# Weights, gated buffers and batch rows at other addresses in a fused FFT filter and gated feed-forward kernel

## The chip, the cores and the metric

The kernel runs on one core of a Trainium2 chip. The metric is the device time of one launch in microseconds. Before the change it is 1562.73 us, the median of three runs (1562.23 to 1562.77).

A core has five engines that the text names: TensorE (PE in the profile, its weight loads PEld), VectorE (DVE), ScalarE (ACT), GpSimd (POOL) and SyncE (SP, which issues most DMAs). SBUF is the on-chip memory of 128 partitions that all engines read. PSUM holds what PE accumulates.

## The reference

The input `x` has 8 batches of 3136 rows of 256 values. A filter is applied in the frequency domain along the rows, and the result goes through a gated feed-forward layer with a convolution of width 3 over the hidden rows:

```python
X = np.fft.rfft(x, axis=1)
y = np.fft.irfft(X * (filt_r + 1j * filt_i), n=3136, axis=1)
h = np.maximum(y @ w_in, 0.0)              # 256 -> 1024
conv = sum(conv_w[k] * hp[:, k:k + S, :] for k in range(3))
gate = 1.0 / (1.0 + np.exp(-conv))
out = (h * gate) @ w_out                   # 1024 -> 256
```

`hp` is `h` with a row of zeros at either end. `conv_w` has a weight per hidden feature and tap.

## The kernel before

**First stage** (until about 365 us). The transforms are matrix products with tables, in fp32. For each batch and pair of rows, PE runs L323, L334 (a transpose), L346 or L349, and L233. DVE multiplies with the filter (L358 to L360), POOL adds (L362), and the result goes through DRAM (`b_dram`) and comes back as `br`. The last table product (L215) gives `y`, transposed, in PSUM. ACT copies it to `y0` in fp32r, a 32-bit format in which PE needs one pass for a matmul, and DVE writes the remainder to `y1` (`last_out`, L146 and L149). In the same stage the weights are converted. `convert_weights` takes `w_in` and `w_out` in eight pieces; for each, ACT writes the leading part (`wi0`, `wo0`) and POOL the remainder (`wi1`, `wo1`, L152).

**Gated stage** (the rest). Rows are taken in chunks `j` of 896, two halves `i` of 448 in each, and for every chunk the 1024 hidden features in eight slices `f` of 128. One step `m` of the loop is one (j, f, i):

- `inner` (L454): six matmuls on 450 columns into a PSUM tile `ps_h`. For each of two halves `k` of the 256 features, `mm3` runs `wi0` with `y0` (L177), `wi0` with `y1` (L178), `wi1` with `y0` (L179). The `wi` slice is the weights that are loaded, and the `y` row is the operand that moves.
- `relu`, `conv`, `gate` (L465 to L478): ACT and DVE make the gated value `t`.
- `split_g` (L480): ACT writes its leading part to a buffer `g0`, POOL the remainder to `g1` (L152).
- `project` (L488): for each tile of 128 rows three matmuls on 256 columns into `po`: `g0` with `wo0` (L498), `g0` with `wo1` (L499), `g1` with `wo0` (L500). Here the `g` slice is loaded and the `wo` slice moves. Four tiles go with i = 0, three with i = 1.

The next batch's `y` is made between, in 14 pieces per batch (L215 and `last_out`). The order on the four compute engines is the order of this code, step by step (`manual_schedule`). `project` runs six steps behind `inner`.

**Where operands lie.** Pools place their tiles one after another in SBUF. An address here is a byte within a partition, the same on every partition. The table gives the remainder mod 256 of where each slice or row starts in the built program, before and after the change. Before, a slice of `wi` takes 512 bytes and one of `wo` 1024, so all slices have one remainder. A row `k` of a `y` tile takes 3138 x 4 = 12552 bytes, which is 8 above a multiple of 256. A half of 448 columns is 1792 bytes, a multiple of 256, and a `g` slice of 128 is 512 bytes, so neither changes a remainder.

| operand | before | after |
|---|---|---|
| `wi0`, `wi1`, slice f | 160 | 160 + 32 f |
| `wo0`, slice f | 160 | 160 + 32 f |
| `wo1`, slice f | 160 | 32 + 32 f |
| `y0`, rows k = 0, 1, even batch | 160, 168 | 192, 0 |
| `y1`, rows k = 0, 1, even batch | 192, 200 | 64, 128 |
| `y0`, rows k = 0, 1, odd batch | 160, 168 | 160, 224 |
| `y1`, rows k = 0, 1, odd batch | 192, 200 | 32, 96 |
| `g0`, by buffer | 224 (four) | 160, 0, 96, 192, 32 |
| `g1`, by buffer | 224 (four) | 128, 224, 64, 160, 0 |

Of the kernel before, what the change touches and what calls it, by code (L numbers as in the profile page):

```python
# [9 lines left out]
F32 = mybir.dt.float32  # L10
F32R = mybir.dt.float32r
# [5 lines left out]
S = 3136  # L17
# [3 lines left out]
D = 256  # L21
FF = 1024
KT = D // 128
NF = FF // 128
SUB = 448
# [99 lines left out]
def tile_fft_filter_gated_ffn(  # L125
# [16 lines left out]
    nc = tc.nc  # L142
    B = x.shape[0]

    def hi_act(dst, src):
        nc.scalar.activation(dst, src, AF.Copy)  # L146
# [4 lines left out]
    def lo_pool(dst, src, hi):  # L151
        nc.gpsimd.tensor_tensor(out=dst, in0=src, in1=hi.bitcast(F32), op=ALU.subtract)  # L152

    def to_f32(dst, raw, e, m):


        v = nc.vector
        pairs = raw.rearrange("p (n t) -> p n t", t=2)
        low, high = pairs[:, :, 0].bitcast(U32), pairs[:, :, 1]
        v.tensor_scalar(e, high, 3, 0x3FFFFFF8, op0=ALU.logical_shift_left, op1=ALU.bitwise_and)  # L160
        yield
        v.tensor_scalar(m, high, 30, 30, op0=ALU.logical_shift_right, op1=ALU.logical_shift_left)
        yield
        v.tensor_tensor(out=e, in0=e, in1=m, op=ALU.bitwise_or)
        yield
        v.tensor_scalar(m, high, 27, 0xF, op0=ALU.logical_shift_right, op1=ALU.bitwise_and)
        yield
        v.scalar_tensor_tensor(out=dst, in0=m, scalar=7.0, in1=e.bitcast(F32), op0=ALU.is_ge, op1=ALU.mult)
        yield
        v.tensor_scalar(e, dst.bitcast(I32), 23, 23, op0=ALU.logical_shift_right, op1=ALU.logical_shift_left)  # L170
        yield
        v.scalar_tensor_tensor(out=e.bitcast(F32), in0=low, scalar=2.0**-52, in1=e.bitcast(F32), op0=ALU.mult, op1=ALU.mult)
        yield
        nc.gpsimd.tensor_tensor(out=dst, in0=dst, in1=e.bitcast(F32), op=ALU.add)

    def mm3(ps, wh, wl, rh, rl, start=True, stop=True, **kw):
        nc.tensor.matmul(ps, lhsT=wh, rhs=rh, start=start, stop=False, **kw)  # L177
        nc.tensor.matmul(ps, lhsT=wh, rhs=rl, start=False, stop=False, **kw)  # L178
        nc.tensor.matmul(ps, lhsT=wl, rhs=rh, start=False, stop=stop, **kw)  # L179
# [4 lines left out]
    wc = ctx.enter_context(tc.tile_pool(name="wc", bufs=1))  # L184
# [1 line left out]
    cw = wc.tile([128, 3, NF], F32, name="cw")  # L186
    nc.gpsimd.memset(cw[:, 0, 0:1], 0.0)
    nc.scalar.activation(cw[:, 0, 0:1], cw[:, 0, 0:1], AF.Sigmoid)
    wi = [wc.tile([128, KT, FF], F32R, name=f"wi{h}") for h in range(2)]
    wo = [wc.tile([128, NF, D], F32R, name=f"wo{h}") for h in range(2)]  # L190


    ys, yps = {}, []
# [6 lines left out]

    def y_slices(b, sl):
        if sl.start == 0:
            ys[b] = [yps[b % 2].tile([128, KT, S + 2], F32R, name=f"y{h}") for h in range(2)]
            for t in ys[b]:
                nc.gpsimd.memset(t[:, :, 0:1].bitcast(F32), 0.0)
                nc.gpsimd.memset(t[:, :, S + 1:S + 2].bitcast(F32), 0.0)
        return (t[:, :, 1:S + 1].rearrange("p k (a c) -> p k c a", c=N2)[:, :, sl] for t in ys[b])
# [10 lines left out]
    def last_out(b, c):  # L218
        yh, yl = y_slices(b, slice(c, c + 2))
        pv = lasts.pop((b, c))[:, 0:4 * N1].rearrange("p (k c a) -> p k c a", c=2, a=N1)  # L220
        hi_act(yh, pv)
        lo_dve(yl, pv, yh)
# [5 lines left out]
    parts = {}  # L228
# [16 lines left out]
    with (  # L245
# [36 lines left out]
        def load_weights(k):  # L282
            raws[k] = raw = cv.tile([128, 2, 512], I32, name="raw")
            for part, src in enumerate((w_in, w_out)):
                nc.sync.dma_start(out=raw[:, part], in_=src[:, 512 * k:512 * k + 512])
# [6 lines left out]
        def convert_weights():  # L292

            for k in range(8):
                raw = raws.pop(k)
                em = cv.tile([128, 2, 512], I32, name="em", bufs=1)
                ws = cv.tile([128, 2, 256], F32, name="ws")
                yield from to_f32(ws.rearrange("p t n -> p (t n)"), raw.rearrange("p t n -> p (t n)"), em[:, 0], em[:, 1])
                yield
                parts = [[t.rearrange("p a b -> p (a b)")[:, 256 * k:256 * k + 256] for t in w] for w in (wi, wo)]  # L300
                for part, (wh, wl) in enumerate(parts):
                    hi_act(wh, ws[:, part])
                yield
                for part, (wh, wl) in enumerate(parts):
                    lo_pool(wl, ws[:, part], wh)
                yield
                if k < 6:
                    load_weights(k + 2)
# [68 lines left out]
        for i in range(XBUFS):  # L377
            load_first(i)
        csteps, wsteps = convert_conv(), convert_weights()
        done = NP * B + 1  # L380
        NI = done + N2 // 2 + 2
# [57 lines left out]
    wp = ctx.enter_context(tc.tile_pool(name="wp", bufs=2, reuse_waits="tile"))  # L439
# [4 lines left out]
    hs, ts, gs, pos = {}, {}, {}, {}  # L444
# [8 lines left out]

    def inner(j, f, i):  # L454
        ps = ps_h.tile([128, 512], F32, name="ps_h")[:, 0:SUB + 2]
        fs = slice(128 * f, 128 * f + 128)
        b, u = divmod(2 * j + i, NSUB)
        us = slice(u * SUB, u * SUB + SUB + 2)
        for k in range(KT):
            mm3(ps, wi[0][:, k, fs], wi[1][:, k, fs], ys[b][0][:, k, us], ys[b][1][:, k, us], start=k == 0, stop=k == KT - 1)  # L460
        hs[j, f, i] = ps

    def relu(j, f, i):
# [16 lines left out]
    def split_g(j, f, i):  # L480
        t = ts.pop((j, f, i))
        if i == 0:
            gs[j, f] = [wp.tile([128, 2 * SUB], F32R, name=f"g{h}", bufs=4) for h in range(2)]
        gh, gl = (g[:, i * SUB:i * SUB + SUB] for g in gs[j, f])
        hi_act(gh, t)
        lo_pool(gl, t, gh)

    def project(j, f, i):  # L488
        gh, gl = gs[j, f]
        if f == 0 and i == 0:  # L490
            pos[j] = [ps_o.tile([128, 512], F32, name=f"po{k}") for k in range(4)], wp.tile([128, NT, D], F32, name="ot")
        po, ot = pos[j]
        tiles = range(4) if i == 0 else range(4, NT)
        for t in tiles:
            o = po[t // 2][:, t % 2 * D:t % 2 * D + D]
            sl = slice(128 * t, 128 * t + 128)
            first, last = f == 0 and t % 2 == 0, f == NF - 1
            nc.tensor.matmul(o, lhsT=gh[:, sl], rhs=wo[0][:, f], start=first, stop=False, skip_group_check=True)  # L498
            nc.tensor.matmul(o, lhsT=gh[:, sl], rhs=wo[1][:, f], start=False, stop=False, skip_group_check=True)  # L499
            nc.tensor.matmul(o, lhsT=gl[:, sl], rhs=wo[0][:, f], start=False, stop=last, skip_group_check=True)  # L500

    def evacuate(j, f, i):
        if f < NF - 1:
# [17 lines left out]
    for b in range(1, B):  # L521
        start = ((NSUB * (b - 1) - 1) // 2 + 1) * 16 + (4 if b == 1 else 0)
        stop = NSUB * b // 2 * 16 + NSUB * b % 2
# [3 lines left out]
    with tc.manual_schedule(engines=COMPUTE):  # L527
        for m in range(NH + PLAG):
            if m + 4 in pieces:
                last_load(*pieces[m + 4])  # L530
            if a := at(m):
                inner(*a)
            if m in pieces:
                last_stage(*pieces[m], ps_h.tile([128, 512], F32, name="ps_h"))
            if 1 <= m < 4:
                pt = ps_o.tile([128, 512], F32, name=f"po{m}")[0:112].rearrange("p (n d) -> p n d", n=2)
                third(B - 1, NP - 4 + m, pt)
            if a := projected(m):
                project(*a)
            if a := at(m - 1):  # L540
                relu(*a)
                conv(*a)
            if a := at(m - 2):
                gate(*a)
            if a := at(m - 3):
                split_g(*a)
            if m in pieces:
                last_out(*pieces[m])
            if 1 <= m < 4:
                store(B - 1, NP - 4 + m, pt)  # L550
            if a := projected(m):
                evacuate(*a)
# [44 lines left out]
```

## Time and profile before

| | before |
|---|---|
| median of three runs | 1562.73 us |
| the profiled execution | 1559.94 us |
| its span | 1558.2 us |
| ACT busy, 0 to 330 us | 195.42 us |
| POOL busy, 0 to 330 us | 167.59 us |
| PE busy, 330 to 400 us | 64.70 us |

The profile is one execution. Its span runs from the first to the last instruction of the program, and the execution's own time stands beside it. In a row of the groups, "L177 PE MATMUL ps_h<-y,wi" names the line, the engine, the operation, what is written and what is read, then the shape, the number of instructions, their busy time in us, the mean length of one in ns, and the idle time of the engine before them with what ended it. Matmuls overlap: the record of one runs on beyond the start of the next. A row of the timeline gives start and length in us. A row of the chain of waits does the same for a piece of the work that ended last.

### The profile page before, as it was taken

How to read it: one execution, taken by the hardware profiler on the slowest of the kernel's cores; microseconds unless marked ns; L12 is line 12 of the kernel's file. 1: busy time of each engine (PE TensorE's matmuls, PEld its weight loads, DVE VectorE, ACT ScalarE, POOL GpSimd, SP SyncE). 2: the span in 40 equal slices, each digit the busy share in tenths (PEclk: the TensorE clock that was granted, in tenths of full speed). 3: DMA queues.
4: the chain of work that ended last, by engine and by line, in shares of the span. 5: the costliest groups of instructions: out<-in, count | busy, mean ns of one | idle time of the engine just before them, and what ended most of it. 6: DMA issues, size and time to landing. Idle time of an engine off the chain costs nothing.

```text
span 1558.2 us, 27801 instructions
## 1 busy us (share of the span) xinstructions
PE 1537.8 (99%) x10320; PEld 1418.2 (91%) x10320; DVE 1297.0 (83%) x1978; ACT 1245.0 (80%) x2274; POOL 703.0 (45%) x625
## 2 busy tenths in 40 slices
PE   8999999998999999999999999999999999999998
PEld 7787778877999999999999999999999999999998
DVE  3888888788888888888888888888888888888887
ACT  5655555566888888888888888888888888888887
POOL 3455555533444444444444444444444434444444
PEclk9999999999999999999999999999999999999999
DMA  9855555452111011111111011111011110100001
GB/s 236 261 179 168 172 169 164 137 148 78 33 52 48 31 47 48 49 49 47 48 42 36 27 53 52 44 48 48 31 48 42 49 54 27 46 25 25 24 25 48
DMA packets 89062, 115.24 MB, mean 74 GB/s; under 512 B 7400, under 2 KB 60168, under 8 KB 88928
## 3 DMA queue, kind: packets, MB, share of 16 engines
q1 hardware_dynamic: 74592, 87.77, 18.4%
q10 hardware_dynamic: 14336, 25.70, 5.8%
q8 instruction: 82, 1.34, 0.4%
q14 instruction: 52, 0.43, 0.1%
HBM read 62.06 MB, written 51.38 MB: 73 GB/s over the span
## 4 chain that ended last, share of the span: by engine, by line
PE 94%; DMA 2%; DVE 1%; ACT 1%; issue 0%; SPq 0%; POOL 0%; ACTq 0%; POOLq 0%; DVEq 0%
PE ps_h L178 12%; PE ps_h L179 12%; PE ps_h L177 11%; PE po L498 11%; PE po L500 11%; PE po L499 11%; PE ps L233 6%; PE ps_h L215 5%; PE pp L346 5%; PE ps L323 5%; PE ps L334 3%; DMA x<-in_x 1%; PE ps L215 1%; DVE y L149 1%; ACT y L146 0%; PE pp L349 0%
## 5 line engine op out<-in xcount | busy, mean ns | idle before, releaser
L152 POOL TENSOR_TENSOR g<-t,g 128x448 fp32r<-128x448 f32 x448 | 517.1, 1154 | 663.5 <-ACT g L146 259.3
L498 PE MATMUL po<-wo,g 128*128 128x256 f32 x1568 | 441.4, 282 | 0.0
L500 PE MATMUL po<-wo,g 128*128 128x256 f32 x1568 | 433.9, 277 | 0.4 <-POOL g L152 0.4
L499 PE MATMUL po<-wo,g 128*128 128x256 f32 x1568 | 433.4, 276 | 0.0
L472 DVE SCALAR_TENSOR_TENSOR t<-ps_h,cw,t 128x448 f32<-128x448 f32 x448 | 305.7, 682 | 85.6 <-ACT t L467 75.2
L178 PE MATMUL ps_h<-y,wi 128*128 128x450 f32 x896 | 330.3, 369 | 5.6 <-DVE y L149 5.6
L177 PE MATMUL ps_h<-y,wi 128*128 128x450 f32 x896 | 329.1, 367 | 3.3 <-DVE t L478 1.9
L179 PE MATMUL ps_h<-y,wi 128*128 128x450 f32 x896 | 328.8, 367 | 0.0
L473 DVE SCALAR_TENSOR_TENSOR t<-ps_h,cw,t 128x448 f32<-128x448 f32 x448 | 306.5, 684 | 16.0
L467 ACT ACTIVATE t<-ps_h,cw 128x448 f32<-128x448 f32 x448 | 284.8, 636 | 43.2 <-ACT ps_h L465 2.6
L498 PEld LDWEIGHTS po<-wo,g 128*128 128x128 f32 x1568 | 294.8, 188 | 7.1
L499 PEld LDWEIGHTS po<-wo,g 128*128 128x128 f32 x1568 | 294.3, 188 | 5.7
L500 PEld LDWEIGHTS po<-wo,g 128*128 128x128 f32 x1568 | 294.5, 188 | 0.6 <-POOL g L152 0.6
L465 ACT ACTIVATE ps_h<-ps_h 128x450 f32<-128x450 f32 x448 | 251.8, 562 | 32.9 <-PE ps_h L179 27.0
L478 DVE TENSOR_TENSOR t<-ps_h,t 128x448 f32<-128x448 f32 x448 | 275.3, 615 | 0.1
L477 ACT ACTIVATE t<-t 128x448 f32<-128x448 f32 x448 | 255.0, 569 | 12.4 <-DVE t L473 11.2
L146 ACT ACTIVATE g<-t 128x448 fp32r<-128x448 f32 x448 | 254.7, 568 | 0.2 <-DVE t L478 0.2
L362 POOL TENSOR_TENSOR z<-u,v 120x512 f32<-120x512 f32 x112 | 156.6, 1398 | 184.3 <-DVE v L360 154.1
L178 PEld LDWEIGHTS ps_h<-y,wi 128*128 128x128 f32 x896 | 168.3, 188 | 14.7 <-DVE y L149 7.9
L179 PEld LDWEIGHTS ps_h<-y,wi 128*128 128x128 f32 x896 | 168.3, 188 | 13.9
L177 PEld LDWEIGHTS ps_h<-y,wi 128*128 128x128 f32 x896 | 169.9, 190 | 11.7 <-DVE t L478 2.9
L149 DVE TENSOR_TENSOR y<-ps_h,y 128x448 fp32r<-128x448 f32 x98 | 103.1, 1053 | 75.3 <-ACT y L146 75.3
(62 smaller groups left out, 1661.6 us busy)
## 6 DMA issues: line engine op xcount, KB each, us to landing
x<-in_x SPq DMA_DIRECT2D x112, 224.0 KB, 2.9
b_dram<-sb ACTq DMA_DIRECT2D x112, 224.0 KB, 2.3
br<-b_dram SPq DMA_DIRECT2D x112, 224.0 KB, 2.6
out<-ot SPq DMA_DIRECT2D x27, 896.0 KB, 4.1
raw<-in_w_in SPq DMA_DIRECT2D x8, 256.0 KB
raw<-in_w_out SPq DMA_DIRECT2D x8, 256.0 KB
t_sb<-in_fr SPq DMA_DIRECT2D x15, 112.0 KB
t_sb<-in_fi SPq DMA_DIRECT2D x14, 112.0 KB
```

Of the source, the lines that this page charges most:

```text
L152: nc.gpsimd.tensor_tensor(out=dst, in0=src, in1=hi.bitcast(F32), op=ALU.subtract)
L177: nc.tensor.matmul(ps, lhsT=wh, rhs=rh, start=start, stop=False, **kw)
L178: nc.tensor.matmul(ps, lhsT=wh, rhs=rl, start=False, stop=False, **kw)
L179: nc.tensor.matmul(ps, lhsT=wl, rhs=rh, start=False, stop=stop, **kw)
L467: nc.scalar.activation(t, h[:, 1:SUB + 1], AF.Copy, scale=cw[:, 1, f:f + 1])
L472: nc.vector.scalar_tensor_tensor(out=t, in0=h[:, 0:SUB], scalar=cw[:, 0, f:f + 1], in1=t, op0=ALU.mult, op1=ALU.add)
L473: nc.vector.scalar_tensor_tensor(out=t, in0=h[:, 2:SUB + 2], scalar=cw[:, 2, f:f + 1], in1=t, op0=ALU.mult, op1=ALU.add)
L477: nc.scalar.activation(t, t, AF.Sigmoid)
L478: nc.vector.tensor_mul(t, h[:, 1:SUB + 1], t)
L498: nc.tensor.matmul(o, lhsT=gh[:, sl], rhs=wo[0][:, f], start=first, stop=False, skip_group_check=True)
L499: nc.tensor.matmul(o, lhsT=gh[:, sl], rhs=wo[1][:, f], start=False, stop=False, skip_group_check=True)
L500: nc.tensor.matmul(o, lhsT=gl[:, sl], rhs=wo[0][:, f], start=False, stop=last, skip_group_check=True)
```

## The change

Four things change, all of them places in SBUF.

- `wi` tiles get 136 elements for each slice of 128, and `wo` tiles 264 for 256: 32 bytes of gap behind each slice. A pad of 128 bytes follows each `wo` tile.
- A row of `y` gets a pitch of S + 16 in place of S + 2 elements, and a pad of 32 bytes goes behind the first pair of `y` tiles in their pool.
- `g` tiles get 24 more elements, and there are five of each in place of four.
- The conversion of weights writes through the new shape: a piece of `wi` is two slices.

```diff
-    wi = [wc.tile([128, KT, FF], F32R, name=f"wi{h}") for h in range(2)]
-    wo = [wc.tile([128, NF, D], F32R, name=f"wo{h}") for h in range(2)]
+    wi = [wc.tile([128, KT, NF, 136], F32R, name=f"wi{h}") for h in range(2)]
+    wo = []
+    for h in range(2):
+        wo.append(wc.tile([128, NF, D + 8], F32R, name=f"wo{h}"))
+        wc.tile([128, 32], F32, name=f"pad{h}")
...
-            ys[b] = [yps[b % 2].tile([128, KT, S + 2], F32R, name=f"y{h}") for h in range(2)]
+            ys[b] = [yps[b % 2].tile([128, KT, S + 16], F32R, name=f"y{h}") for h in range(2)]
+            if b == 0:
+                yps[0].tile([128, 8], F32, name="pad_y")
...
-                parts = [[t.rearrange("p a b -> p (a b)")[:, 256 * k:256 * k + 256] for t in w] for w in (wi, wo)]
-                for part, (wh, wl) in enumerate(parts):
-                    hi_act(wh, ws[:, part])
+                f = k % 4 * 2
+                parts = [[t[:, k // 4, f:f + 2, 0:128] for t in wi], [t[:, k, 0:D] for t in wo]]
+                values = [ws[:, 0].rearrange("p (f n) -> p f n", f=2), ws[:, 1]]
+                for (wh, wl), v in zip(parts, values):
+                    hi_act(wh, v)
...
-            mm3(ps, wi[0][:, k, fs], wi[1][:, k, fs], ys[b][0][:, k, us], ys[b][1][:, k, us], start=k == 0, stop=k == KT - 1)
+            mm3(ps, wi[0][:, k, f, 0:128], wi[1][:, k, f, 0:128], ys[b][0][:, k, us], ys[b][1][:, k, us], start=k == 0, stop=k == KT - 1)
...
-            gs[j, f] = [wp.tile([128, 2 * SUB], F32R, name=f"g{h}", bufs=4) for h in range(2)]
+            gs[j, f] = [wp.tile([128, 2 * SUB + 24], F32R, name=f"g{h}", bufs=5) for h in range(2)]
...
-            nc.tensor.matmul(o, lhsT=gh[:, sl], rhs=wo[0][:, f], start=first, stop=False, skip_group_check=True)
+            nc.tensor.matmul(o, lhsT=gh[:, sl], rhs=wo[0][:, f, 0:D], start=first, stop=False, skip_group_check=True)
```

The instructions of PE, ACT, DVE and SP are the same, in the same order and with the same waits. On POOL the waits of the `g1` writes move. Before, at the start of the gated stage (a row is an instruction, with the semaphores that it waits for; a number behind a name tells tiles apart, and each `g` pair of a chunk and slice has a number of its own):

```order
L205 MEMSET y_3937 128x2
L206 MEMSET y_3937 128x2
L205 MEMSET y_3938 128x2 [waits DMAHW6_49,PE_49,Pool_49]
L206 MEMSET y_3938 128x2
L152 TENSOR_TENSOR g_3969<-t,g_3968 128x448 [waits Activation_49] x2
L152 TENSOR_TENSOR g_4033<-t,g_4032 128x448 [waits PE_49,Activation_49,Pool_49]
L152 TENSOR_TENSOR g_4033<-t,g_4032 128x448 [waits Activation_49]
```

The fourth pair is written without a wait for PE, and from the fifth on the first write of each pair waits for PE. The same place on POOL after the change:

```order
L210 MEMSET y_3940 128x2
L211 MEMSET y_3940 128x2
L210 MEMSET y_3941 128x2 [waits DMAHW6_49]
L211 MEMSET y_3941 128x2
L152 TENSOR_TENSOR g_3972<-t,g_3971 128x448 [waits Activation_49] x2
L152 TENSOR_TENSOR g_4036<-t,g_4035 128x448 [waits Activation_49] x2
L152 TENSOR_TENSOR g_4100<-t,g_4099 128x448 [waits PE_49,Activation_49,Pool_49]
```

The wait for PE begins one pair later, since the fifth pair has a buffer of its own. One early wait for the first stage moves from the memset of `y` to the second `g` pair.

More of the change, by code (lines that the diff above doesn't have):

```diff
@@ L299, in convert_weights @@
                 yield
-                parts = [[t.rearrange("p a b -> p (a b)")[:, 256 * k:256 * k + 256] for t in w] for w in (wi, wo)]
-                for part, (wh, wl) in enumerate(parts):
-                    hi_act(wh, ws[:, part])
+                f = k % 4 * 2
[3 more added lines that the diff above has]
+                    hi_act(wh, v)
                 yield
-                for part, (wh, wl) in enumerate(parts):
-                    lo_pool(wl, ws[:, part], wh)
+                for (wh, wl), v in zip(parts, values):
+                    lo_pool(wl, v, wh)
                 yield
@@ L455, in inner @@
         ps = ps_h.tile([128, 512], F32, name="ps_h")[:, 0:SUB + 2]
-        fs = slice(128 * f, 128 * f + 128)
         b, u = divmod(2 * j + i, NSUB)
@@ L497, in project @@
             first, last = f == 0 and t % 2 == 0, f == NF - 1
-            nc.tensor.matmul(o, lhsT=gh[:, sl], rhs=wo[0][:, f], start=first, stop=False, skip_group_check=True)
-            nc.tensor.matmul(o, lhsT=gh[:, sl], rhs=wo[1][:, f], start=False, stop=False, skip_group_check=True)
-            nc.tensor.matmul(o, lhsT=gl[:, sl], rhs=wo[0][:, f], start=False, stop=last, skip_group_check=True)
+            nc.tensor.matmul(o, lhsT=gh[:, sl], rhs=wo[0][:, f, 0:D], start=first, stop=False, skip_group_check=True)
+            nc.tensor.matmul(o, lhsT=gh[:, sl], rhs=wo[1][:, f, 0:D], start=False, stop=False, skip_group_check=True)
+            nc.tensor.matmul(o, lhsT=gl[:, sl], rhs=wo[0][:, f, 0:D], start=False, stop=last, skip_group_check=True)
     def evacuate(j, f, i):
```

## The prediction

> **What bounds the kernel now.** I read the page's busy times and the chain that ended last first, because a change of addresses can only matter on the engine that sets the end.
>
> ```profile
> PE 1537.8 (99%) x10320; PEld 1418.2 (91%) x10320; DVE 1297.0 (83%) x1978; ACT 1245.0 (80%) x2274; POOL 703.0 (45%) x625
> PE 94%; DMA 2%; DVE 1%; ACT 1%; issue 0%; SPq 0%; POOL 0%; ACTq 0%; POOLq 0%; DVEq 0%
> PE ps_h L178 12%; PE ps_h L179 12%; PE ps_h L177 11%; PE po L498 11%; PE po L500 11%; PE po L499 11%; PE ps L233 6%; PE ps_h L215 5%; PE pp L346 5%; PE ps L323 5%; PE ps L334 3%; DMA x<-in_x 1%; PE ps L215 1%; DVE y L149 1%; ACT y L146 0%; PE pp L349 0%
> ```
>
> TensorE is busy 99% of the span, and 94% of the chain is TensorE. 35% of the chain is the inner product (L177 to L179), 33% the projection (L498 to L500). The table by stretches shows that this holds throughout the gated stage:
>
> ```profile
> 400.00:700.00 300.00, 298.81 (x2089) 287.18 (x2089) 256.82 (x396) 259.74 (x479) 129.95 (x121) 1.00 0.15 45
> 1000.00:1300.00 300.00, 298.82 (x2087) 287.08 (x2086) 256.57 (x395) 260.30 (x480) 129.57 (x121) 1.00 0.14 44
> ```
>
> The columns after the stretch and its length are PE, its weight loads (PEld), DVE, ACT and POOL. PE lacks 1.2 us in 300. ACT is busy for 260 (87%), DVE for 257, POOL for 130. So the stage from 400 us to the end is a stream of matmuls whose spacing alone is the time. ACT would take over only if PE shortened by some 13%. The granted clock is 1.00, so no throttle is involved.
>
> ```profile
> L177 PE MATMUL ps_h<-y,wi 128*128 128x450 f32 x896 | 329.1, 367 | 3.3 <-DVE t L478 1.9 <-ACT y L146 1.2
> L178 PE MATMUL ps_h<-y,wi 128*128 128x450 f32 x896 | 330.3, 369 | 5.6 <-DVE y L149 5.6
> L179 PE MATMUL ps_h<-y,wi 128*128 128x450 f32 x896 | 328.8, 367 | 0.0
> L498 PE MATMUL po<-wo,g 128*128 128x256 f32 x1568 | 441.4, 282 | 0.0
> L499 PE MATMUL po<-wo,g 128*128 128x256 f32 x1568 | 433.4, 276 | 0.0
> L500 PE MATMUL po<-wo,g 128*128 128x256 f32 x1568 | 433.9, 277 | 0.4 <-POOL g L152 0.4
> ```
>
> There are 3x896 = 2688 inner matmuls and 3x1568 = 4704 projection matmuls. Idle time before them is under 10 us in all. The 367 and 276 ns are lengths of overlapping records. What counts is the spacing of the starts, which the timeline of PE shows:
>
> ```profile
> 901.25 0.37 PE L177 MATMUL ps_h<-y,wi 128*128 128x450 f32 x1
> 901.45 0.36 PE L178 MATMUL ps_h<-y,wi 128*128 128x450 f32 x1
> 901.65 0.37 PE L179 MATMUL ps_h<-y,wi 128*128 128x450 f32 x1
> 901.86 0.36 PE L177 MATMUL ps_h<-y,wi 128*128 128x450 f32 x1
> 902.06 0.37 PE L178 MATMUL ps_h<-y,wi 128*128 128x450 f32 x1
> 902.27 0.36 PE L179 MATMUL ps_h<-y,wi 128*128 128x450 f32 x1
> 902.47 0.28 PE L498 MATMUL po<-wo,g 128*128 128x256 f32 x1
> ...
> 903.38 0.28 PE L500 MATMUL po<-wo,g 128*128 128x256 f32 x1
> 903.49 0.37 PE L177 MATMUL ps_h<-y,wi 128*128 128x450 f32 x1
> ...
> 904.72 0.28 PE L498 MATMUL po<-wo,g 128*128 128x256 f32 x1
> ```
>
> Six inner matmuls take 1.22 us, then nine projections 1.02, then six inner again 1.23. That is 204 ns for an inner matmul and 113 ns for a projection. As a check, 2688 x 0.204 + 4704 x 0.113 = 548 + 532 = 1080 us, the bulk of the span after the first stage.
>
> **The change part by part.** No matmul, copy or transfer is added, and every engine issues the same work in the same order. What changes is where operands lie. So the question is whether 204 and 113 ns depend on addresses. The next rows give one group of six inner matmuls, each row from a stretch of a few ns, in the order in which they run (903.49 to 904.72 us):
>
> ```profile
> L177 PE MATMUL ps_h<-y,wi 128*128 128x450 f32 x1 | 0.4, 368 | 0.0
> L178 PE MATMUL ps_h<-y,wi 128*128 128x450 f32 x1 | 0.4, 365 | 0.0
> L179 PE MATMUL ps_h<-y,wi 128*128 128x450 f32 x1 | 0.4, 367 | 0.0
> L177 PE MATMUL ps_h<-y,wi 128*128 128x450 f32 x1 | 0.4, 363 | 0.0
> L178 PE MATMUL ps_h<-y,wi 128*128 128x450 f32 x1 | 0.4, 369 | 0.0
> L179 PE MATMUL ps_h<-y,wi 128*128 128x450 f32 x1 | 0.4, 365 | 0.0
> ```
>
> The six differ in nothing but operand addresses. Mod 256 their moving rows start at 160, 192, 160, 168, 200, 168, while the weights loaded meanwhile for the next matmul start at 160 (for the sixth, a `g` slice, at 224). So addresses do count, but in these six by 6 ns from best to worst. Slow are the two whose moving row starts where the weights start (368, 367) and the row at 200 (369). The others are 365, 363, 365, mean 364.3. The mean of all six is 366.2.
>
> *Inner product.* After the change all rows are on multiples of 32, none at 168 or 200, and the weights' start moves by 32 with each f. A moving row meets weights of its own remainder at one f of eight. I give such a meeting 367.5, as now, and all others 364.3: 7/8 x 364.3 + 1/8 x 367.5 = 364.7. That is 1.5 ns less than 366.2, and 2688 x 1.5 = **-4.0 us**. Distances such as 64, 96 or 128 are not among the six rows, so this is a choice, and both ends stay open. At best, all that exceeds the bare stream goes. The fp32 rows give that stream:
>
> ```profile
> 318.08 0.87 PE pp L346 x2
> 319.39 0.86 PE ps L233 x4
> 321.64 0.88 PE ps L215 x8
> 67.01 0.88 PE ps L323 x8
> ```
>
> L346 streams 512 columns in 0.435 us, and L233 256 columns in 0.215: 0.85 ns for a column in fp32. The projection's 256 columns of fp32r take 113 ns, about half of that, so a bare fp32r column is 0.42 ns and 450 columns are 191 ns (an estimate from these rows). Against 204 that is -13 ns, or -35 us. At worst every inner matmul is like the row with 369: +2.8 ns, or +7.5 us.
>
> *Projection.* `wo` moves with f, `wo1` lies 128 off `wo0`, and the five `g` buffers have five remainders. L215 and L323 load 128 columns of weights, as a projection does, and stream only 112 (95 ns at 0.85). They still take 110 ns each, so the load paces them. 113 is 3 ns above that, so at most 4704 x 3 = -14 us can go. Nothing says that it does: a projection's weights lie 64 off its moving row now, and the last of a group, whose next weights (`wi`) have its own remainder, takes the same 113 (starts 903.38 and 903.49). I take 0. The upper end is 3 ns, half the spread of the six, on each: +14 us.
>
> *Fifth buffer.* It only moves POOL's wait for PE by one tile:
>
> ```profile
> POOL g L152 <- PE ps_h L179: 75.6, 58, 1.4
> PE po L500 <- POOL g L152: 0.4, 1, 0.4
> ```
>
> POOL may lose up to 76 us of waits, but PE waited for POOL only 0.4 us in the whole run. Worth 0 to -1 us; I take 0. The other engines' waits are the same, so what was hidden stays hidden.
>
> *Split of the weights.* ACT and POOL write each 256-wide piece of `wi` as two runs of 128.
>
> ```profile
> L152 POOL TENSOR_TENSOR wi<-ws,wi x8: 720/730/742, 112.1 to 301.2; 128x256 fp32r<-128x256 f32 x8
> ```
>
> The eight POOL instructions for `wi`, 0.73 us each, lie beside the first stage, where PE is bound by itself. I count 0, and at worst 1 us if one of them delayed a filter product.
>
> *y pitch.* The first pieces of a batch expose two copies:
>
> ```profile
> 497.83 1.07 ACT y L146
> 498.93 1.02 DVE y L149
> ```
>
> Their stride of 28 elements stays, so 0. A tenth more on seven batches would be 7 x 0.2 = 1.5 us.
>
> The sum is -4.0 us on the profiled span of 1558.2 us: 1554.2. The profiled run took 1559.9 us with what lies around the span, and the median shown is 1562.7. Against that median the forecast is **1558.7 us**.
>
> **The rivals.** *Addresses don't matter on average.* The six rows may differ by their place in the group (first, middle, last weight), not by address; a spread over all remainders then gives the mean of now: 1562.7, within 1.5 us. For it speaks that L323 takes 110 ns whichever of its rows of `s1_sb` is read, and that the projection has the same 113 at two distances. Against it, 365 and 369 are both L178 in the middle of three. The Trainium skill ("TensorE: Matmul & The Clock Gate", Step-by-step: what each phase is for) says that the streaming operand and the weight load have independent read ports, so that loading the next weights takes nothing from the running matmul. By that rule the time would be the 1562.7 of this rival. The trace does not settle it: the 6 ns speak against, the equal 113 for it.
>
> *The stream and the weight load hinder each other, and spread addresses end most of it.* For it: an inner matmul carries 13 ns over the bare stream, and all six distances measured now are small (0 to 40, and 56). If distances from 64 to 192, half of all, lose the 13 ns: 0.5 x 13 x 2688 = -17 us, and with 0.5 ns on each projection -2 us: **1543**. Against it, six remainders changed only 6 of 204 ns.
>
> *Slower: the projection now has the good distance.* Its 64 is kept by every group today (wo at 160, g at 224), and 113 is only 3 ns over the load. With five `g` remainders against eight of `wo`, pairs that hinder each other appear. At 3 ns on half of 4704 it is +7 us, and with no gain in the inner product **1570**. It decides as soon as the projection loses more than 4.0/4704 = 0.9 ns on average. Against it is the equal 113 at distance 0.
>
> **How the numbers follow.** The measurement can tell about 0.2% (3.1 us) from no change. The small gain of the forecast has 0.34, no effect 0.20, the large gain 0.26, slower 0.20. The forecast's own -4.0 us lies close to the limit, so two thirds of its chance (0.22) count as faster and 0.12 as the same. The large gain adds 0.26 to faster: 0.48. Same: 0.12 + 0.18 of "no effect" = 0.30. Slower: 0.20 + 0.02 = 0.22. The ends are 1562.7 - 50 = 1513 (all 35 + 14 us gained) and 1562.7 + 23 = 1586 (7.5 + 14 + 1.5 us). The range reaches past both rivals but not to these ends: 1536 to 1572. The likeliest case alone would be 1554 to 1562.
>
> **What would show it.** In the profile after, the starts of six inner matmuls: 1.21 to 1.22 us for the forecast, 1.23 for no effect, 1.18 or less for the large gain, with records that differ from f to f. Nine projections at 1.02 us bear out the zero; 1.04 or more is the slower rival. POOL's wait for PE should shrink from 75.6 us without a trace in PE. The forecast is wrong if distances from 64 to 192 behave unlike the ones the six rows show, or if a transfer or copy at a batch's start waits for something that it doesn't wait for now.

## The result and the profile after

| | before | after |
|---|---|---|
| median of four runs | 1562.48 us (1558.58 to 1562.77) | 1582.98 us (1581.67 to 1584.73) |
| ratio, with its 95% interval | | 1.0138 (1.0118 to 1.0157) |
| profiled execution, its span | 1559.94, 1558.2 us | 1582.27, 1580.5 us |
| mean spacing of the projection's matmuls | 113.5 ns | 118.1 ns |
| mean spacing of the inner product's matmuls | 204.7 ns | 205.2 ns |

The change makes the kernel 20.5 us slower, outside the predicted range. The last two rows are worked out from the starts of PE's matmuls in the trace: for each, the time to the next start. Left out are spacings over 150 and 230 ns, that is the first projection behind a piece of L215 (about 202 ns in both kernels) and the few that a wait or the start of the gated stage holds up; 4601 of 4704 projections and about 2660 of 2688 inner matmuls remain. All means of this kind below are taken so. The groups of the page after, as they stood before (columns: shape, count, busy us, mean ns of one, idle time ahead):

```profile
PE 1559.0 (99%) x10320; PEld 1438.6 (91%) x10320; DVE 1294.6 (82%) x1978; ACT 1246.7 (79%) x2274; POOL 702.9 (44%) x625
PE 94%; DVE 2%; DMA 2%; ACT 1%; issue 0%; POOL 0%; SPq 0%; ACTq 0%; POOLq 0%; DVEq 0%
L177 PE MATMUL ps_h<-y,wi 128*128 128x450 f32 x896 | 330.0, 368 | 3.2 <-DVE t L484 1.8
L178 PE MATMUL ps_h<-y,wi 128*128 128x450 f32 x896 | 330.0, 368 | 5.5 <-DVE y L149 5.5
L179 PE MATMUL ps_h<-y,wi 128*128 128x450 f32 x896 | 329.2, 367 | 0.0
L504 PE MATMUL po<-wo,g 128*128 128x256 f32 x1568 | 448.3, 286 | 0.0
L505 PE MATMUL po<-wo,g 128*128 128x256 f32 x1568 | 440.1, 281 | 0.0
L506 PE MATMUL po<-wo,g 128*128 128x256 f32 x1568 | 440.7, 281 | 0.4 <-POOL g L152 0.4
```

PE is still 99% busy, its share of the chain is 94% as before, and it waits for nothing new. DVE, ACT and POOL have the busy time of before within 2.4 us. What grew is PE itself, by 21.2 us: the three projection lines (L504 to L506, before L498 to L500) have records 4 to 5 ns longer, the inner lines at most 1 ns. The table by stretches (stretch, its length, PE with its instructions, PEld, DVE, ACT, POOL, clock) says that no wait entered and the clock did not fall:

```profile
400.00:700.00 300.00, 298.85 (x2051) 287.33 (x2050) 252.47 (x388) 255.62 (x470) 128.34 (x119) 1.00 0.14 44
1000.00:1300.00 300.00, 298.85 (x2049) 287.24 (x2048) 251.46 (x387) 255.38 (x469) 127.52 (x119) 1.00 0.14 43
```

PE is busy for 298.85 us of 300, as it was, but gets 2051 matmuls done in place of 2089. The same matmuls are slower, in every stretch alike. The timeline of PE shows one round:

```profile
924.63 0.37 PE L177 MATMUL ps_h<-y,wi 128*128 128x450 f32 x1
...
925.86 0.28 PE L504 MATMUL po<-wo,g 128*128 128x256 f32 x1
925.98 0.28 PE L505 MATMUL po<-wo,g 128*128 128x256 f32 x1
926.09 0.28 PE L506 MATMUL po<-wo,g 128*128 128x256 f32 x1
...
926.80 0.28 PE L506 MATMUL po<-wo,g 128*128 128x256 f32 x1
926.92 0.28 PE L504 MATMUL po<-wo,g 128*128 128x256 f32 x1
```

Six inner matmuls take 1.23 us, as before. Nine projections take 1.06 us, before 1.02. On 4704 projections 4.6 ns are 21.6 us. The exact sums say the same: of the 22.3 us of more span, the spacings of all projections account for 21.3, those of the inner matmuls with the waits between them for -0.3, and everything else, above all the first stage, for the rest. The time went into the spacing of the projections. The experiments ask what sets it.

### The profile page after: what moved, and what is told of

Its sections match the earlier page's. It is cut to its first block, busy times and chain, and to the rows that moved or that the text cites. A ratio compares the mean times of both kernels' runs of the same rounds, so it can differ in the third digit from the quotient of the medians.

```text
span 1580.5 us, 27800 instructions
## 1 busy us (share of the span) xinstructions
PE 1559.0 (99%) x10320; PEld 1438.6 (91%) x10320; DVE 1294.6 (82%) x1978; ACT 1246.7 (79%) x2274; POOL 702.9 (44%) x625
## 4 chain that ended last, share of the span: by engine, by line
PE 94%; DVE 2%; DMA 2%; ACT 1%; issue 0%; POOL 0%; SPq 0%; ACTq 0%; POOLq 0%; DVEq 0%
PE ps_h L178 12%; PE po L504 12%; PE po L506 11%; PE ps_h L179 11%; PE po L505 11%; PE ps_h L177 11%; PE ps L238 6%; PE ps_h L220 5%; PE ps L330 5%; PE pp L353 5%; PE ps L341 3%; DMA x<-in_x 1%; PE ps L220 1%; DVE y L149 1%; ACT y L146 0%; PE pp L356 0%
## 5 line engine op out<-in xcount | busy, mean ns | idle before, releaser
L504 PE MATMUL po<-wo,g 128*128 128x256 f32 x1568 | 448.3, 286 | 0.0
L506 PE MATMUL po<-wo,g 128*128 128x256 f32 x1568 | 440.7, 281 | 0.4 <-POOL g L152 0.4
L505 PE MATMUL po<-wo,g 128*128 128x256 f32 x1568 | 440.1, 281 | 0.0
L504 PEld LDWEIGHTS po<-wo,g 128*128 128x128 f32 x1568 | 295.8, 189 | 5.9
L506 PEld LDWEIGHTS po<-wo,g 128*128 128x128 f32 x1568 | 295.2, 188 | 0.6 <-POOL g L152 0.6
L149 DVE TENSOR_TENSOR y<-ps_h,y 128x448 fp32r<-128x448 f32 x98 | 103.0, 1051 | 86.5 <-ACT y L146 86.5
```

The lines of the kernel that those rows point to most:

```text
L504: nc.tensor.matmul(o, lhsT=gh[:, sl], rhs=wo[0][:, f, 0:D], start=first, stop=False, skip_group_check=True)
L505: nc.tensor.matmul(o, lhsT=gh[:, sl], rhs=wo[1][:, f, 0:D], start=False, stop=False, skip_group_check=True)
L506: nc.tensor.matmul(o, lhsT=gl[:, sl], rhs=wo[0][:, f, 0:D], start=False, stop=last, skip_group_check=True)
```

## The experiments

All edits are to the kernel before. Except for the last two kernels, each figure is one run, shown beside one run of the kernel before on the same chip; the kernel before ranged from 1558.6 to 1564.4 us over all runs, so a difference under 6 us between two single runs can be none; there the spacings tell more than the time. The expectations name theories by a letter. A: the remainder of the moving `wo` row counts. B: the loaded `g` slice or its fifth buffer. C: any variation from matmul to matmul breaks a steady pattern. D: the place in SBUF as such. E: the distance between the slice that is loaded and the row that moves meanwhile sets a value. H: at the good distance there are two rhythms of the projections, chosen by what ran before. J: each distance has its own value, and the changed kernel averages them. K: variation costs something on top. "Distance" is the start of the `g` slice less that of the `wo` row, mod 256; before it is 224 - 160 = 64 for every projection but the last of a group, during which a `wi` slice is loaded (160 - 160 = 0).

### One part of the change at a time

`wo` alone (e1_wo; the conversion of the weights and the reads of `wo` follow the new shape):

```diff
-    wo = [wc.tile([128, NF, D], F32R, name=f"wo{h}") for h in range(2)]
+    wo = []
+    for h in range(2):
+        wo.append(wc.tile([128, NF, D + 8], F32R, name=f"wo{h}"))
+        wc.tile([128, 32], F32, name=f"pad{h}")
...
```

> Only the output weights: 32 bytes of gap behind each slice of wo and the two pads; wi, y and g as before. Projections stand 113.4 ns apart before and 118.1 after. Theory A (what hurts is that the moving wo rows no longer start at one remainder): 118 ns, about +21 us. Theory B (what hurts is the loaded g slices, by remainder or by the fifth buffer): 113.4, +0. Theory C (any operand whose remainder changes from matmul to matmul breaks a steady pattern, so each part alone does it): 118, +20 us. Theory D (where the g and t region lies, not its remainders): it moves by 768 bytes, 113 to 118. Inner matmuls stay at 204.6 in all.

`g` alone (e2_g):

```diff
-            gs[j, f] = [wp.tile([128, 2 * SUB], F32R, name=f"g{h}", bufs=4) for h in range(2)]
+            gs[j, f] = [wp.tile([128, 2 * SUB + 24], F32R, name=f"g{h}", bufs=5) for h in range(2)]
```

> Only the gated buffers: five of a pitch of 3680 bytes; wi, wo and y as before. Theory A: projections at 113.4 ns, +0. Theory B: 118, +21 us. Theory C: 118, +20 us. Theory D: 113 to 118. Inner matmuls at 204.6.

`wi` alone (e3_wi; conversion and reads again follow the shape):

```diff
-    wi = [wc.tile([128, KT, FF], F32R, name=f"wi{h}") for h in range(2)]
+    wi = [wc.tile([128, KT, NF, 136], F32R, name=f"wi{h}") for h in range(2)]
...
```

> Only the input weights: 32 bytes of gap behind each slice of wi; wo, y and g as before. Theories A and B: projections at 113.4, inner matmuls within 1 ns of 204.6, +0 to +2 us. Theory C: inner matmuls lose their fixed sequence of 205, 203, 206, 203, 208, 204 ns, and the projection next to them stays at 113.4. Theory D: 113 to 118, since everything behind wi moves by 1024 bytes.

`y` alone (e4_y). The larger `y` tiles also push the `g` buffers from 224 to 160, that is to distance 0:

```diff
-            ys[b] = [yps[b % 2].tile([128, KT, S + 2], F32R, name=f"y{h}") for h in range(2)]
+            ys[b] = [yps[b % 2].tile([128, KT, S + 16], F32R, name=f"y{h}") for h in range(2)]
+            if b == 0:
+                yps[0].tile([128, 8], F32, name="pad_y")
```

> Only the batch rows: a pitch of S + 16 and the pad behind the first pair; wi, wo and g keep one remainder each (the g slices all at 160, so loads and moving wo rows now share it). Theories A and B: projections 113.4, +0 us; a distance of 0 is as good as 64. Inner matmuls: fixed sequences, one for even and one for odd batches, with a mean between 202 and 207 (-7 to +6 us). Theory C: the same, since nothing varies from one f to the next. Theory D: 113 to 118.

| kernel | us | before beside it | projection, ns | inner, ns |
|---|---|---|---|---|
| e1_wo | 1580.1 | 1560.8 | 117.8 | 204.7 |
| e2_g | 1584.0 | 1560.8 | 118.6 | 204.8 |
| e3_wi | 1571.4 | 1560.8 | 115.0 | 204.9 |
| e4_y | 1592.0 | 1560.8 | 119.0 | 206.4 |

The groups of the four pages (in this order; the second of the three projection lines, which was 276 before):

```profile
L503 PE MATMUL po<-wo,g 128*128 128x256 f32 x1568 | 439.7, 280 | 0.0
L499 PE MATMUL po<-wo,g 128*128 128x256 f32 x1568 | 440.7, 281 | 0.0
L501 PE MATMUL po<-wo,g 128*128 128x256 f32 x1568 | 435.3, 278 | 0.0
L501 PE MATMUL po<-wo,g 128*128 128x256 f32 x1568 | 442.2, 282 | 0.0
```

Moving `wo` alone or `g` alone costs 19 and 23 us, about the whole loss each, and the two together cost no more. So neither A nor B fits alone; what both edits break is the relation of `g` to `wo`. `e4_y` varies neither, and with `g` at distance 0 throughout has the slowest projections of the four. That speaks against C. `e3_wi` was expected at 113.4 ns by all theories but D, and D allowed it to slow down because everything behind `wi` moves by 1024 bytes. It slowed down, by 10.6 us. Its projections read `wo` and `g` at the remainders of before and still went from 113.5 to 115.0 ns, 6.6 us in all. What changed beside them is the place of the `wi` slices, which the inner matmuls and the last projection of each group load; more on this below.

### All distances alike

Four kernels give every moving row the remainder 160 and every loaded slice (160 + D) mod 256, so that each matmul of both kinds has the distance D:

```diff
+    wc.tile([128, D // 4], F32, name="pad_wi")    # ahead of wi; none for D = 0
...
+    wc.tile([128, (256 - D) // 4], F32, name="pad_wo")    # ahead of wo; none for D = 0
...
-            ys[b] = [yps[b % 2].tile([128, KT, S + 2], F32R, name=f"y{h}") for h in range(2)]
+            ys[b] = [yps[b % 2].tile([128, KT, S + 64], F32R, name=f"y{h}") for h in range(2)]
+            if b == 0:
+                yps[0].tile([128, 16], F32, name="pad_y")
...
+    wp.tile([128, D // 4], F32, name="pad_g", bufs=1)    # ahead of g; none for D = 0
```

> All moving rows (y rows of both batches' parities, both wo) start at 160 mod 256 and all loaded slices (wi, g) at 160 too: one distance, 0, from the moving row to the weights loaded meanwhile, everywhere. Theory E (the spacing settles to a value set by that distance, and changing distances keep it from settling): projections settle at 120 ns as in the y run, inner matmuls at one constant value; about +30 us for the projections, -5 to +10 us for the inner ones. Theory C (only variation costs): projections 113.4, inner constant, 0 to -10 us.

> Moving rows all at 160, loaded slices all at 224: distance 64 everywhere. Theory E: projections 113.4 ns as in the kernel before, inner matmuls at one constant value somewhere between 198 and 211 (the values seen so far), so between -18 and +17 us. Theory C: projections 113.4, the same as at distance 0.

> Moving rows all at 160, loaded slices all at 32: distance 128 everywhere. Theory E: projections constant at a value of their own (112 to 122), inner constant; total between -20 and +45 us. Theory C: projections 113.4, as at 0 and 64.

> Moving rows all at 160, loaded slices all at 96: distance 192 everywhere. Theory E: projections constant at a value of their own (112 to 122); if the pattern repeats at 128 as it does at 256, then as with 64: 113.4. Inner constant. Theory C: projections 113.4.

| kernel | us | before beside it | projection, ns | inner, ns |
|---|---|---|---|---|
| u0 | 1583.0 | 1561.6 | 119.6 | 203.6 |
| u64 | 1582.6 | 1561.6 | 117.4 | 206.1 |
| u128 | 1584.2 | 1561.6 | 118.8 | 204.9 |
| u192 | 1586.2 | 1561.6 | 118.2 | 205.5 |

All four are as slow as the changed kernel although nothing varies in them: C falls. `u0` bears on the prediction directly. At distance 0 throughout, projections take 120 ns and not 113, while the inner product has its lowest mean of all kernels, 203.6 ns. But `u64` has the distance of before and is slow as well, so distance alone (E) isn't all. Its trace shows two rhythms. The groups of two stretches of its PE, first 884.30 to 884.70 us, the fifth to tenth projections behind a piece of L215 (the fifth, an L504, is still slow), then 901.97 to 903.03, nine projections behind an inner group:

```profile
L504 PE MATMUL po<-wo,g 128*128 128x256 f32 x2 | 0.6, 278 | 0.0
L505 PE MATMUL po<-wo,g 128*128 128x256 f32 x2 | 0.6, 276 | 0.0
L503 PE MATMUL po<-wo,g 128*128 128x256 f32 x2 | 0.6, 276 | 0.0
```

```profile
L503 PE MATMUL po<-wo,g 128*128 128x256 f32 x3 | 0.8, 281 | 0.0
L504 PE MATMUL po<-wo,g 128*128 128x256 f32 x3 | 0.8, 281 | 0.0
L505 PE MATMUL po<-wo,g 128*128 128x256 f32 x3 | 0.8, 281 | 0.0
```

A projection's record is its spacing and about 163 ns more, so 276 is a spacing of 113 and 281 one of 118. At one and the same distance, the first run comes down to the 113 of before, and the second stays at 118. What differs is what ran ahead.

### Undoing parts

`e5_y_g224` is e4_y with `g` put back to 224. `e6_g160` is the kernel before with nothing but `g` moved to 160. `e7_g5` has the fifth buffer at the old pitch, so all stay at 224. `e8_yflat` puts all `y` rows to 160, as in the four kernels above, and keeps `g` at 224.

```diff
+    wp.tile([128, 16], F32, name="pad_g", bufs=1)    # e5_y_g224 and e8_yflat
+    wp.tile([128, 48], F32, name="pad_g", bufs=1)    # e6_g160
...
-            gs[j, f] = [wp.tile([128, 2 * SUB], F32R, name=f"g{h}", bufs=4) for h in range(2)]
+            gs[j, f] = [wp.tile([128, 2 * SUB], F32R, name=f"g{h}", bufs=5) for h in range(2)]    # e7_g5
...
+            ys[b] = [yps[b % 2].tile([128, KT, S + 64], F32R, name=f"y{h}") for h in range(2)]    # e8_yflat
```

> The y run again, with 64 bytes of pad ahead of the gated buffers, so that the g slices stay at 224 and every projection has the operands of the kernel before (mod 256). Theory H (two regimes: the same projection runs at 113 or at 118 ns, and what the inner matmuls ahead of it leave decides): projections begin at 113 behind an L215 piece and sit at 117 to 119 behind most inner groups, about +20 us. Theory E (only the projection's own distance counts): 113.4 throughout, and the y run's 119 came from g at 160; then only the inner change is left, 0 to +7 us.

> The kernel before with 192 bytes of pad ahead of the gated buffers alone: g at 160 in place of 224 (four buffers, one remainder), rows of y, wi and wo as before. Theory E: 120 ns, +30 us, as in the two runs with g at 160. Theory H: the fast regime may hold, since the inner matmuls are those of before: 113.4 with all but the last of the six inner ones unchanged, 0 us; 120 speaks for E.

> The kernel before with five gated buffers of the old pitch of 3584 bytes: all ten at 224. Only the fifth buffer is tried. Theories E and H, and theory A: projections 113.4, inner 204.7, 0 us (within 1.5); POOL's wait for PE falls from 76 us to under 60. Theory B with the fifth buffer itself as the cause: 118, +20 us.

> All y rows at 160 (pitch S + 64 and a pad), wi at 160, g at 224, wo at 160: the projection's operands as before, the inner product as in the run with one distance of 0, which had 203.6 ns. Theory E: projections 113.4, inner 203.6: -3 us. Theory H: 113.4 only if these inner matmuls happen to leave the state that the fast regime needs; otherwise 117 to 118, about +17 us.

| kernel | us | before beside it | projection, ns | inner, ns |
|---|---|---|---|---|
| e5_y_g224 | 1574.4 | 1562.4 | 115.8 | 205.4 |
| e6_g160 | 1586.0 | 1562.4 | 118.6 | 205.0 |
| e7_g5 | 1559.5 | 1562.4 | 113.5 | 204.7 |
| e8_yflat | 1567.0 | 1562.4 | 115.5 | 203.9 |

`e6_g160` is the plainest of all: 192 bytes of pad ahead of `g`, and no other edit, cost 23.6 us. No weight has a gap and no batch row has moved. The pad also moves the tiles `t` and `ot` of the same pool, which other engines use. They are not the cause: in `e1_wo` and in `d80` below `t` and `ot` stay at 224 and the projections are slow. `e7_g5` clears the fifth buffer; POOL's wait for PE, 58 times as before, didn't shrink:

```profile
L499 PE MATMUL po<-wo,g 128*128 128x256 f32 x1568 | 433.4, 276 | 0.0
POOL g L152 <- PE ps_h L179: 75.5, 58, 1.4
```

`e5` and `e8` keep distance 64 in the projection and move only `y`, which the projection doesn't read. Behind an inner group, `e5` settles at 113 in odd batches and stays near 117.5 in even ones, which differ in where the `y` rows lie. One of the three lines in an odd batch (893.30 to 893.62 us) and in an even one (1058.75 to 1059.00 us):

```profile
L502 PE MATMUL po<-wo,g 128*128 128x256 f32 x2 | 0.6, 276 | 0.0
L502 PE MATMUL po<-wo,g 128*128 128x256 f32 x2 | 0.6, 281 | 0.0
```

Behind a piece of L215 it is the other way round: mostly 113 in even batches, 117.5 in odd ones. `e8` reaches 113 in nearly all groups, after a slow start that repeats alike in those behind inner matmuls: 122, 118, 119, 116, 114, 113 ns. `e3_wi` fits in here: its projections settle at 113 too, but behind inner matmuls their first four spacings are 117, 117, 116 and 116 ns on average, where the kernel before has 112 or 113. The matmuls ahead choose how, and whether, the projections get to 113: H is borne out, without a rule for the choice.

### The other distances

`g` alone is moved, as in e6_g160, to distances 32, 96, 160 and 224:

```diff
+    wp.tile([128, 56], F32, name="pad_g", bufs=1)    # p32; 8 in p96, 24 in p160, 40 in p224
```

> The kernel before with a pad ahead of the gated buffers alone: g slices at 192, distance 32 in every projection but the last of a group. Theory J (each distance has a value of its own and the changed kernel averages them): the mean of all eight settled values comes out at 118 within 1; with 120, 113.3, 119.4 and 117.7 for 0, 64, 128 and 192, the four new ones average 118 to 119, about +20 us each. Theory K (variation costs on top): the new ones lie mostly at 112 to 114, 0 us.

> The same with g slices at 0, distance 96. Theory J: the four new distances average 118 to 119 ns. Theory K: mostly 112 to 114.

> The same with g slices at 64, distance 160. Theory J: the four new distances average 118 to 119 ns. Theory K: mostly 112 to 114.

> The same with g slices at 128, distance 224. Theory J: the four new distances average 118 to 119 ns. Theory K: mostly 112 to 114.

| kernel | us | before beside it | projection, ns | inner, ns |
|---|---|---|---|---|
| p32 | 1582.4 | 1561.1 | 118.0 | 205.4 |
| p96 | 1582.4 | 1561.1 | 117.7 | 205.0 |
| p160 | 1588.2 | 1561.1 | 119.5 | 205.0 |
| p224 | 1582.5 | 1561.1 | 117.5 | 205.1 |

The last 72 projections of each kernel run with no inner product between them, long enough to settle. The groups of PE in a stretch of 5.2 us of it (one of the three lines each), for distances 0 (e6_g160), 32 (p32), 64 (before), 96 (p96), 128 (u128), 160 (p160), 192 (u192), 224 (p224):

```profile
L500 PE MATMUL po<-wo,g 128*128 128x256 f32 x15 | 4.2, 283 | 0.0
L500 PE MATMUL po<-wo,g 128*128 128x256 f32 x15 | 4.2, 281 | 0.0
L499 PE MATMUL po<-wo,g 128*128 128x256 f32 x16 | 4.4, 276 | 0.0
L500 PE MATMUL po<-wo,g 128*128 128x256 f32 x16 | 4.5, 280 | 0.0
L504 PE MATMUL po<-wo,g 128*128 128x256 f32 x15 | 4.2, 281 | 0.0
L499 PE MATMUL po<-wo,g 128*128 128x256 f32 x15 | 4.2, 283 | 0.0
L504 PE MATMUL po<-wo,g 128*128 128x256 f32 x15 | 4.2, 279 | 0.0
L500 PE MATMUL po<-wo,g 128*128 128x256 f32 x15 | 4.2, 281 | 0.0
```

From the starts of the tenth to the 66th of the 72, the mean settled spacings are 120.0, 118.3, **113.3**, 117.4, 118.6, 120.0, 117.8 and 117.8 ns. (At 160, for one, they repeat as 118, 121, 117, 125, 116, 123; at 0 each is 120.) Only 64 is good, and even it not always: `u64` stays at 117.8 through this stretch too, so the slower rhythm lasts once it is entered. Whether another distance has a faster rhythm that none of these runs entered stays open. The mean of the eight is 117.9 ns, and the changed kernel, whose projections go through all eight about equally often, has 118.1. That looks like J, but the agreement is luck, for J fails matmul by matmul. In the changed kernel the means by own distance all lie between 117.7 and 118.5 ns: 64 has 118.4 there in place of 113.3, and 0 has 118.0 in place of 120.0. Where the distance changes each time, the good one isn't fast and the bad one isn't slowest. So K is right for 64 and wrong for 0.

### Distance 64 elsewhere, and a finer step

`s64` moves `wo` to 192 and `g` to 0, which keeps 64. `d80` leaves `wo` and reads and writes each `g` slice 16 bytes further on. Both were timed in three rounds.

```diff
+    wc.tile([128, 8], F32, name="pad_wo")     # s64, ahead of wo
+    wc.tile([128, 56], F32, name="pad_end")   # s64, behind wo
+    wp.tile([128, 8], F32, name="pad_g", bufs=1)    # s64
...
+            gs[j, f] = [wp.tile([128, 2 * SUB + 64], F32R, name=f"g{h}", bufs=4) for h in range(2)]    # d80
+        gh, gl = (g[:, 4 + i * SUB:4 + i * SUB + SUB] for g in gs[j, f])    # d80
+            sl = slice(4 + 128 * t, 4 + 128 * t + 128)    # d80
```

> The kernel before with wo rows moved from 160 to 192 and g slices from 224 to 0: the projection's distance stays 64; wi and y as before. If the distance counts: projections settle at 113.3 ns, entered with or without a few slow ones (the last inner matmul and the last projection of a group have other distances now), 0 to +12 us. If the remainders themselves count: 117 to 120, about +20 us.

> The kernel before with every g slice 16 bytes further on (at 240, distance 80). If the good place is wide (more than 16 bytes on this side): projections at 111.7 to 113.4, -8 to 0 us. If it is narrow: 115 to 119, +8 to +25 us.

| kernel | us, median of four | ratio to before | projection, ns | inner, ns |
|---|---|---|---|---|
| s64 | 1571.8 | 1.0064 (1.0045 to 1.0082) | 114.9 | 206.0 |
| d80 | 1588.7 | 1.0176 (1.0157 to 1.0195) | 118.6 | 206.4 |

The groups of the same closing stretch, s64 and then d80:

```profile
L502 PE MATMUL po<-wo,g 128*128 128x256 f32 x16 | 4.4, 276 | 0.0
L499 PE MATMUL po<-wo,g 128*128 128x256 f32 x15 | 4.2, 280 | 0.0
```

With both operands moved and the distance kept, the settled 113.3 is back. With the distance off by 16 bytes it is 118.7. So it is the distance that admits 113, and neither remainder by itself: `wo` at 160 gives 113 or not as `g` moves, and `g` at 0 gives it with `wo` at 192 but not with `wo` at 160 (`p96`). A, B and D fall as causes of the settled value. That the same distance does the same rests on these two pairs, 160 with 224 and 192 with 0. `s64` is still 10 us slower than before. Its projections start each group slowly (the timeline of PE; the first spacings are 0.12, not 0.11):

```profile
900.52 0.28 PE L501 MATMUL po<-wo,g 128*128 128x256 f32 x1
900.64 0.28 PE L502 MATMUL po<-wo,g 128*128 128x256 f32 x1
900.76 0.28 PE L503 MATMUL po<-wo,g 128*128 128x256 f32 x1
...
901.55 0.28 PE L501 MATMUL po<-wo,g 128*128 128x256 f32 x1
901.66 0.28 PE L502 MATMUL po<-wo,g 128*128 128x256 f32 x1
901.78 0.28 PE L503 MATMUL po<-wo,g 128*128 128x256 f32 x1
```

On average the first three spacings of a group behind inner matmuls are 122, 116 and 114 ns. Over the trace its projections take 6.2 us more than before, and its inner matmuls, 1.3 ns slower each, 3.0 us more. In the kernel before, groups behind inner matmuls start at 112 or 113 ns at once (behind a piece of L215 the one of 202 ns is followed by 122, 116, 114): besides the good distance, it has inner matmuls that lead straight into 113. No kernel here beats it; `e7_g5` lies within its scatter.

## Why the prediction was wrong

- **The bound** was right: a stream of matmuls whose spacing is the time, before and after.
- **The projection, "I take 0", is the step that failed.** It measured +4.6 ns on 4704, +21.6 us, nearly the whole loss. The trace of before had one distance for nearly all projections, and the step took one matmul per group, the last, which meets distance 0 at 113 ns, as proof that distance doesn't count. But a matmul amid others doesn't show the value of its own distance: `e6_g160` starts its groups behind inner matmuls at 118, 119, 118, 117 and is steady at 120 only from the tenth on, which a group of nine doesn't have, and in the changed kernel no matmul shows its own distance's value. The upper end of +14 us, 3 ns from the spread of the inner rows, was also too small; `u0` and `e6_g160` settle 6.7 ns above before. The argument that at most 3 ns could be gained stands, since no kernel here settled below 113.3; it should have said as well that the kernel sat close to the best value, and that a move of address could then hardly do other than lose.
- **The inner product** was forecast at -1.5 ns and measured +0.5, +1.5 us in place of -4.0. Its reading of the six rows (equal remainders slow) falls with `u0`: all distances 0, and the lowest inner mean, 203.6 ns. The rows differ by order and history too, as the text had said of its rival. It also took distances without their sign, and for the projection 64 and 192, which differ in sign alone, give 113.3 and 117.8 ns.
- **The fifth buffer** at nothing was right (`e7_g5`). That POOL's wait would shrink was wrong, without harm: it is 75.5 us in `e7_g5`, as before, and 97.3 us (73 times) in the changed kernel, and PE still waits for POOL 0.4 us.
- **The split of the weights and the pitch of y** cost nothing that shows by itself: the copies of L149 take 1.05 us each in both kernels, and the projections alone account for 21.3 of 22.3 us.
- **The rivals.** "The projection now has the good distance" was the right mechanism: the group of nine went from 1.02 to 1.06 us, past the 1.04 that the text had named. Its break-even of 0.9 ns stands. Its price, 3 ns on half the projections, had to be 4.6 ns on all: in the changed kernel every projection is slow, whatever its own distance. "Addresses don't matter on average" falls. The rule behind it, which the Trainium skill states ("TensorE: Matmul & The Clock Gate", Step-by-step: what each phase is for), that loading the next weights takes no read bandwidth from the running matmul, gave no ground for an effect of addresses. The runs show one: the same matmuls settle at 113.3 or 120.0 ns by nothing but the place of `g`. Whether the load holds up the stream or the stream the load, the runs don't show. "Spread addresses end the hindrance" falls: of the distances it called good, those from 64 to 192, the inner product, on which it put its price, takes 206.1, 204.9 and 205.5 ns at 64, 128 and 192, more than the 203.6 at 0, and for the projection only 64 is good.
- **The range** ended at 1572, although the text's own upper end was 1586. That end would have held the result, but by luck: it had 14 us for the projection, which lost 21, and 7.5 us for the inner product, which lost at most 1.5. The end also leaves out the text's own 1 us for the weights.

## What to carry to other kernels

Where PE's spacing is the time and a short matmul sits within a few ns of what its weight load allows, its operand addresses are part of the tuning: here a pad of 192 bytes ahead of one buffer cost 1.5%. Before spreading addresses, look whether the present ones are good: a settled spacing near the floor of the trace (L215 and L323, 110 ns by the rows shown) can hardly do better; none of the kernels here did. And any edit that resizes a tile may shift its neighbours: `e4_y` moved `g` without naming it.

## What the runs showed of the hardware

- The spacing of 128x256 fp32r matmuls, each with weights of its own, depends on the distance between the slice that is loaded and the row that moves: 113.3 ns at 64, and 117.4 to 120.0 at 0, 32, 80, 96, 128, 160, 192 and 224 (mod 256).
- Distances 256 apart gave the same: `g` lies 256 bytes further in `e5_y_g224` than in the kernel before, and both settle at 113.3; it lies 768 further in `u0` than in `e6_g160`, and both settle at 120.0. Distances 128 apart did not (64 and 192, 0 and 128).
- At distance 64 there are two rhythms, 113 and 118 ns. Which one a group enters depends on the matmuls ahead of it (`u64`, `e5_y_g224`), and that of 113 takes up to five slower ones to reach (`e8_yflat`); that of 118 can last through 72.
- The inner product's mean moved only from 203.6 to 206.4 ns over all address patterns tried.

What in the chip makes the distance matter isn't shown, nor what chooses the rhythm. A period of 256 rests on the two pairs above. Steps finer than 16 bytes, and distances under 64 other than 0 and 32, weren't tried.
